# A Fourier filter with a two-layer network: the complex product M by three real products, and the units of a step behind its first layer

## The chip, the cores and the metric

The kernel runs on one core of one Trainium2 chip. The metric is the time of one execution in device microseconds. A core has the engines TensorE (PE in the profile, its weight loads PEld), VectorE (DVE), ScalarE (ACT), GpSimd (POOL) and SyncE (SP, which here only issues transfers), and 16 DMA engines. TensorE writes to PSUM only; GpSimd works on SBUF.

## The reference

The input x has 8 batches of 3008 rows and 256 columns. A Fourier transform along the rows is mixed by a complex 256 x 256 matrix, shrunk towards zero and transformed back; the result goes through a network with an ELU.

```python
X = np.fft.rfft(x, axis=1)
Yr = Xr @ w_r - Xi @ w_i + b_r
Yi = Xr @ w_i + Xi @ w_r + b_i
Yr = np.sign(Yr) * np.maximum(np.abs(Yr) - lam, 0.0)   # lam = 0.01, Yi alike
y = np.fft.irfft(Yr + 1j * Yi, n=3008, axis=1)
h = y @ w_in                                           # 256 -> 2048
g = np.where(h > 0.0, h, np.exp(np.minimum(h, 0.0)) - 1.0)
out = g @ w_out                                        # 2048 -> 256
```

## The kernel before

**The transform.** 3008 is 47 x 64, so the transform is done in two stages of matmuls each way. For one batch there are five kinds of units. A (6 of them, `unit_A`) is the 64-point stage out of x, which lies in the three tiles `xts`; its result goes to DRAM (tile DA) and comes back in another order as Z (`load_Z`). X (8, `unit_X`) is the 47-point stage, giving XT, real and imaginary parts apart. M (12, `unit_M` with `m_group`) is the complex product with `w_r`, `w_i` for 128 frequencies: four matmuls of 512 columns against `wcat_r` = [w_r, w_i] and `wcat_s` = [-w_i, w_r], then the bias (VectorE, tile yb), the clip and the subtraction (GpSimd, tiles clip and Y), which are the shrinking. B (6, `unit_B`) and Y (8, `unit_Y`) are the two stages back, again with DRAM between them (tile DB, loaded as Bs by `load_Bs`); Y leaves yT, which the network reads. A, X, B and Y are evacuated from PSUM by ScalarE.

**The network.** It goes in steps of 512 rows and 256 of the 2048 hidden columns, 47 steps to a batch (PER), 376 in all. `front` is the first layer (four matmuls, tile hps) and the exponential on ScalarE (tile Et): in one piece, in two halves, or as relu and exponential where the step has an M unit (L737, L738). `elu` takes the minimum of Et with 1: on GpSimd in halves (L763) in steps with no unit, on VectorE (L765) in steps with units other than M, and not at all with M, where the relu does its work. `finish_elu` puts it together with hps into gT on VectorE (L751, L753). `back` is the second layer of the step two before (LAG = 2): eight matmuls of 256 columns in f32 into ps_o, copied out every eighth step (tile osb).

**The order** is written out by hand, and each engine works through its instructions in that order. `plan(b)` gives a batch's 47 steps two lists: units of the next batches (f0) and other work (f1, such as loads of x on GpSimd's queue and of Z and Bs on SyncE's). In each step the loop calls the units of f0, `front`, `finish_elu` for the step before, f1, `elu` and `back`. In step 3 of batch 0 f1 has a `gate` (L599): a one-column copy on GpSimd that waits for a part of Z and so holds back the loads of x that follow it on that queue.

**PSUM.** Units share one buffer (psF, tag fps), which in some steps with no unit also holds an hps; hps has two more buffers (psH), ps_o two (psO). So a unit waits for the evacuation of the one before it, and the first layer of a step for gT of the step two before.

**SBUF.** The three gT buffers are larger than their tiles, which start 0, 32 and 16 bytes into them (`shifted`); the rows of `w_out_r` have 16 unused elements behind them (`E + 16`). Ahead of the steps GpSimd also copies the weights into `wcat_r` and `wcat_s` (L521 to L524) while VectorE makes the matrices of the transform (L488 and its neighbours). Batch 0 runs its units, and batch 1 its A units, before the first step, with VectorE and ScalarE sharing them (`first_M`, L221, keeps the product as it is).

Of the kernel before, what the change touches and what calls it, by code (L numbers as in the profile page):

```python
# [23 lines left out]
NJ = 24  # L24
# [5 lines left out]
def kernel(  # L30
# [31 lines left out]
    wcat_s = constp.tile([P, 2, 2 * D], BF16, name="wcat_s")  # L62
    w_in_s = constp.tile([P, 2, DFF], BF16, name="w_in_s")
    w_out_p = constp.tile([P, NFT, E + 16], F32R, name="w_out_r")
    w_out_r = w_out_p[:, :, 0:E]
    bias_bc = constp.tile([P, 2 * D], F32, name="bias_bc")
    bias_p = constp.tile([P, 2 * D], BF16, name="bias_p")
# [62 lines left out]
    def unit_A(b, u, alone=False, on_dve=False, ahead=False):  # L130
        ci, uu = u // 2, u % 2
        if uu == 0:
            if ahead and ci > 0:
                A_of[b, ci] = shifted(ci - 1, 8 * D, BF16, "A").rearrange("p (n d) -> p n d", d=D)
# [72 lines left out]
    def unit_M(b, q, i):  # L207
        if i == 0:
            mps_of[b, q] = unit_ps("mps", False)
        yb, clip = m_group(b, q, i, mps_of[b, q][:, i, :])  # L210
        nc.gpsimd.tensor_scalar(clip[:], yb, LAM, -LAM, ALU.min, ALU.max)  # L211
        nc.gpsimd.tensor_tensor(Y_of[b, q][:, i, :], yb, clip[:], ALU.subtract)  # L212
# [101 lines left out]
    with tc.tile_pool(name="stagep", bufs=1) as stagep:  # L314
# [35 lines left out]
        w_r_f = row("w_r_f", [P, 2, D])  # L350
        w_i_f = row("w_i_f", [P, 2, D])
# [217 lines left out]
    SHIFT = (0, 32, 16)  # L569

    def shifted(k, n_, dt, name):

        k %= 3
        o = SHIFT[k] * n_ // (8 * TB)
        w_ = n_ + 64 * n_ // (8 * TB)
        t = late1.tile([P, w_], dt, name=name, tag=f"gT{k}")
        return t[:, o : o + n_]
# [31 lines left out]
    load_w_out(0)  # L609
    nc.vector.tensor_scalar(w3[:], v3[:], CMAGIC, -CMAGIC, ALU.add, ALU.add)  # L610
# [134 lines left out]
    def finish_elu():  # L745
        for i, hps, Et, whole, halves in late_elu:
            gT = shifted(i + 2, 2 * TB, F32R, "gT").rearrange("p (s t) -> p s t", s=2)
# [9 lines left out]
    def elu(i, hps, Et, on_pool, on_act):  # L757

        E_ = Et[:]
        if on_pool:  # L760
# [3 lines left out]
        elif not on_act:  # L764
            nc.vector.tensor_scalar(E_, E_, 1.0, -1.0, ALU.min, ALU.add)  # L765
        late_elu.append((i, hps, Et, on_pool or on_act, on_pool))
# [44 lines left out]
    def plan(b):  # L811
# [4 lines left out]
        mid = [("X", u) for u in range(8)] + [  # L816
# [13 lines left out]
        for t, u in enumerate(seq, lead):  # L830
# [9 lines left out]
            if u == ("A", 1):  # L840
                f1[t] += [(load_Bs, (n1, w)) for w in range(4)]
# [68 lines left out]
```

## Time and profile before

| | |
|---|---|
| three timed runs | 917.59, 918.97, 920.98 us; median 918.97 us |
| the profiled execution, first to last instruction (its span) | 916.2 us, 2.8 under the median |
| granted TensorE clock, mean | 0.997 |
| busy: PE, DVE, ACT, POOL | 898.2, 718.1, 696.8, 313.4 us |
| DMA | 106.24 MB, mean 116 GB/s |

The time of the profiled execution is not given apart from its span; so times are worked out on the span, and 2.8 us are put to them for the median of the runs. In the lines of the profile, a group has its source line, engine, operation, output and inputs, shape and count, then the busy time in us and the mean duration in ns, then the time that the engine was idle before it and what ended that. A line of the timeline has its start and duration in us. PE durations contain a latency in which the next matmul already runs, so the distance from start to start is what a matmul occupies.

### The profile page before, as it was taken

How to read it: one execution, taken by the hardware profiler on the slowest of the kernel's cores; microseconds unless marked ns; L12 is line 12 of the kernel's file. 1: busy time of each engine (PE TensorE's matmuls, PEld its weight loads, DVE VectorE, ACT ScalarE, POOL GpSimd, SP SyncE). 2: the span in 40 equal slices, each digit the busy share in tenths (PEclk: the TensorE clock that was granted, in tenths of full speed). 3: DMA queues.
4: the chain of work that ended last, by engine and by line, in shares of the span. 5: the costliest groups of instructions: out<-in, count | busy, mean ns of one | idle time of the engine just before them, and what ended most of it. 6: DMA issues, size and time to landing. Idle time of an engine off the chain costs nothing.

```text
span 916.2 us, 17270 instructions
## 1 busy us (share of the span) xinstructions
PE 898.2 (98%) x6721; PEld 655.8 (72%) x6721; DVE 718.1 (78%) x891; ACT 696.8 (76%) x850; POOL 313.4 (34%) x438
## 2 busy tenths in 40 slices
PE   8889999999999999999999999999999999999997
PEld 3447667876678766886678766787667866777775
DVE  8759778887788777887788877888778877778775
ACT  6658778778778778787787788878877877766664
POOL 6600440323321342405404153033332134343664
PEclk9999999999999999999999999999999999999999
DMA  8997026621284214732266032752228111321011
GB/s 264 310 264 230 24 71 182 210 63 53 70 233 135 71 47 135 191 113 75 65 192 200 24 94 60 218 160 70 70 71 229 30 42 47 87 76 47 26 46 46
DMA packets 90670, 106.24 MB, mean 116 GB/s; under 512 B 5270, under 2 KB 81308, under 8 KB 87228
## 3 DMA queue, kind: packets, MB, share of 16 engines
q1 hardware_dynamic: 84332, 77.62, 30.3%
q0 software_dynamic: 5968, 27.26, 9.0%
q8 instruction: 52, 0.85, 0.4%
q10 hardware_dynamic: 288, 0.26, 0.1%
q14 instruction: 30, 0.25, 0.1%
HBM read 55.32 MB, written 49.81 MB: 115 GB/s over the span
## 4 chain that ended last, share of the span: by engine, by line
PE 88%; DMA 3%; ACT 3%; DVE 3%; issue 1%; SPq 1%; POOL 0%; ACTq 0%; DVEq 0%; POOLq 0%
PE ps_o L784 36%; PE hps L726 34%; PE mps L193 9%; PE xps L176 2%; PE yps L283 2%; PE bps L245 2%; PE aps L145 2%; DMA Bs<-DB 1%; DMA DA<-A 1%; ACT Et L737 1%; ACT Bz L258 1%; SPq L802 0%; DMA xt<-in_x_dram 0%; DVE gT L751 0%; DMA DB<-Bz 0%
## 5 line engine op out<-in xcount | busy, mean ns | idle before, releaser
L784 PE MATMUL ps_o<-w_out_r,gT 128*128 128x256 f32 x3008 | 482.5, 303 | 0.1
L784 PEld LDWEIGHTS ps_o<-w_out_r,gT 128*128 128x128 f32 x3008 | 406.8, 189 | 50.0 <-DVE osb L795 1.0
L726 PE MATMUL hps<-yT,w_in_s 128*128 128x512 bf16 (+4 forms) x1728 | 390.0, 353 | 3.3 <-DVE gT L753 2.5
L751 DVE SCALAR_TENSOR_TENSOR gT<-Et,hps 128x512 fp32r<-128x512 f32 (+1 forms) x272 | 222.8, 848 | 76.3 <-POOL Et L763 39.3
L753 DVE SCALAR_TENSOR_TENSOR gT<-hps,Et 128x1024 fp32r<-128x1024 f32 x198 | 242.1, 1223 | 18.0 <-DMA DA<-A 2.6
L726 PEld LDWEIGHTS <-w_in_s 128*128 128x128 bf16 x1728 | 141.7, 98 | 130.9 <-issue 23.5
L740 ACT ACTIVATE Et<-hps 128x1024 f32<-128x1024 f32 x198 | 203.9, 1030 | 14.3 <-PE hps L726 8.0
L763 POOL TENSOR_SCALAR Et<-Et 128x512 f32<-128x512 f32 x187 | 111.3, 614 | 224.9 <-ACT Et L735 224.9
L765 DVE TENSOR_SCALAR Et<-Et 128x1024 f32<-128x1024 f32 x198 | 137.0, 692 | 49.5 <-ACT Et L740 42.2
L211 POOL TENSOR_SCALAR clip<-yb 128x512 f32<-128x512 f32 x84 | 51.6, 614 | 319.5 <-DVE yb L203 282.1
L735 ACT ACTIVATE Et<-hps 128x512 f32<-128x512 f32 x188 | 102.1, 595 | 65.1 <-PE hps L726 65.1
L737 ACT ACTIVATE Et<-hps 128x1024 f32<-128x1024 f32 x84 | 86.3, 1027 | 72.6 <-PE hps L726 72.1
L212 POOL TENSOR_TENSOR Y<-yb,clip 128x512 bf16<-128x512 f32 x84 | 107.2, 1276 | 7.0
L738 ACT ACTIVATE Et<-Et 128x1024 f32<-128x1024 f32 x84 | 88.8, 1057 | 2.7
L203 DVE TENSOR_TENSOR yb<-mps,bias_bc 128x512 f32<-128x512 f32 x89 | 61.4, 689 | 36.8 <-PE mps L193 29.8
L128 ACT CAST XT<-xps 128x768 bf16<-128x768 f32 x61 | 48.7, 799 | 16.4 <-PE xps L176 16.4
L128 ACT CAST yT<-yps 128x752 bf16<-128x752 f32 x63 | 49.6, 788 | 14.6 <-PE yps L283 14.5
L193 PE MATMUL mps<-wcat_r,XT 128*128 128x512 bf16 x192 | 58.1, 383 | 0.8 <-DVE XT L126 0.4
L128 ACT CAST A<-aps 128x1024 bf16<-128x1024 f32 x45 | 45.5, 1013 | 16.3 <-PE aps L145 14.6
L193 PE MATMUL mps<-wcat_s,XT 128*128 128x512 bf16 x192 | 57.1, 379 | 0.0
L193 PEld LDWEIGHTS <-XT 128*128 128x128 bf16 x384 | 30.8, 98 | 29.9 <-DVE XT L126 0.7
L258 ACT CAST Bz<-bps 128x1024 bf16<-128x1024 f32 x46 | 46.0, 1000 | 2.6 <-PE bps L245 2.6
(110 smaller groups left out, 412.0 us busy)
## 6 DMA issues: line engine op xcount, KB each, us to landing
xt<-in_x_dram POOLq DMA_DIRECT2D x21, 1024.0 KB, 7.1
out_dram<-osb SPq DMA_DIRECT2D x158, 128.0 KB
Bs<-DB SPq DMA_DIRECT2D x32, 384.0 KB
DA<-A SPq DMA_DIRECT2D x21, 512.0 KB
DB<-Bz SPq DMA_DIRECT2D x21, 512.0 KB
Z<-DA SPq DMA_DIRECT2D x7, 1152.0 KB
Z<-DA SPq DMA_DIRECT2D x11, 384.0 KB
xt<-in_x_dram POOLq DMA_DIRECT2D x6, 512.0 KB, 6.2
```

The source lines that it names most:

```text
L128: nc.scalar.copy(dst, src)
L193: nc.tensor.matmul(ps, lhsT=XT[:, dt, c, o : o + P], rhs=wm[:, dt, :], start=(not biased and m == 0 and dt == 0), stop=(m == 1 and dt == 1),)
L212: nc.gpsimd.tensor_tensor(Y_of[b, q][:, i, :], yb, clip[:], ALU.subtract)
L726: nc.tensor.matmul(hps[:, s, c0:c1], lhsT=w_in_s[:, dt, ft * P : ft * P + P], rhs=yT_of[b][:, dt, t0 : t0 + c1 - c0], start=(dt == 0), sto ...
L735: nc.scalar.activation(E_[:, s], hps[:, s], AF.Exp)
L737: nc.scalar.activation(E_, hps[:], AF.Relu, scale=-1.0)
L740: nc.scalar.activation(E_, hps[:], AF.Exp)
L751: nc.vector.scalar_tensor_tensor(o, e, -1.0, h, ALU.add, ALU.max)
L753: nc.vector.scalar_tensor_tensor(o, h, 0.0, e, ALU.max, ALU.add)
L763: eng.tensor_scalar(E_[:, s], E_[:, s], 1.0, 0.0, ALU.min, ALU.max)
L765: nc.vector.tensor_scalar(E_, E_, 1.0, -1.0, ALU.min, ALU.add)
L784: nc.tensor.matmul(po[q][:, i_ % 2, :], lhsT=gT[:, s, i_ * P : i_ * P + P], rhs=w_out_r[:, ft, :], start=(ft == 0 and i_ % 2 == 0), stop=( ...
```

## The change

- **M by three real products**, batches 1 to 7. `unit_D` makes Xd = Xr - Xi (128 frequencies, 256 columns). `unit_M` multiplies Xd by w_i, Xr by w_r - w_i and Xi by w_r + w_i: six matmuls of 256 columns in place of four of 512. Kb = (first product + b_r) is added to the two others on VectorE, which gives the real part and, but for b_i - b_r (tile `bias_d`, added on GpSimd), the imaginary one. The sums of the weights (tile `wsum`) and `bias_d` are made once, on GpSimd, before the first step. Xd for the next unit is made on GpSimd, or on VectorE where the next step has an M too.
- **Order in a step**: `front` comes first and the units of f0 behind it; `finish_elu` now belongs to the same step, at its end. gT of step i is thus given to VectorE in step i and not in i + 1.
- **Order of the units** (`plan`): Y, A or empty steps are put between M units, in batches 5 and 6 behind nearly each, in batch 0 none but B; X starts two steps earlier; the loads of x are at steps 1, 4, 7 in batches 1 to 5, and as before at 3, 8, 13 in batch 0. The first Y units of the next batch come at fixed steps (`due`).
- **Minimum**: on GpSimd in halves wherever neither the two steps before nor the step behind has an M (210 steps for 94), also in steps with X, A, Y or B units; on VectorE in the steps near an M (82 for 198); none in steps with M (84).
- **No padding**: `w_out_r` is dense, and gT starts at its buffer's start (`ring`). `w_r_f` and `w_i_f` lie in the buffers of Y.

```diff
@@ -60,10 +60,11 @@
     M4 = constp.tile([4 * K1, 2 * N1], BF16, name="M4")
     wcat_r = constp.tile([P, 2, 2 * D], BF16, name="wcat_r")
     wcat_s = constp.tile([P, 2, 2 * D], BF16, name="wcat_s")
+    wsum = constp.tile([P, 2, 2, D], BF16, name="wsum")
     w_in_s = constp.tile([P, 2, DFF], BF16, name="w_in_s")
-    w_out_p = constp.tile([P, NFT, E + 16], F32R, name="w_out_r")
-    w_out_r = w_out_p[:, :, 0:E]
+    w_out_r = constp.tile([P, NFT, E], F32R, name="w_out_r")
     bias_bc = constp.tile([P, 2 * D], F32, name="bias_bc")
+    bias_d = constp.tile([P, D], F32, name="bias_d")
     bias_p = constp.tile([P, 2 * D], BF16, name="bias_p")
     lam_n = constp.tile([P, 1], F32, name="lam_n")
     hpi = constp.tile([P, 1], F32, name="hpi")
@@ -131,7 +132,7 @@
         ci, uu = u // 2, u % 2
         if uu == 0:
             if ahead and ci > 0:
-                A_of[b, ci] = shifted(ci - 1, 8 * D, BF16, "A").rearrange("p (n d) -> p n d", d=D)
+                A_of[b, ci] = ring(ci - 1, 8 * D, BF16, "A").rearrange("p (n d) -> p n d", d=D)
             elif alone:
                 A_of[b, ci] = wk4.tile([P, 8, D], BF16, name="A", tag="Bs")
             else:
@@ -204,12 +205,45 @@
         clip = wk2.tile([P, 2 * D], F32, name="clip", tag="clip")
         return yb, clip
 
-    def unit_M(b, q, i):
+    Xd_of = {}
+
+    def unit_D(b, k, eng):
+
+        if k >= NJ // 2:
+            return
+        Xd_of[b, k] = wk2.tile([P, 2, P], BF16, name="Xd", tag="Xd")
+        XT, o = XT_of[b], k * P
+        eng.tensor_tensor(
+            Xd_of[b, k][:], XT[:, :, 0, o : o + P], XT[:, :, 1, o : o + P], ALU.subtract
+        )
+
+    def unit_M(b, q, i, eng):
+
+        k = 2 * q + i
+        XT, Xd, o = XT_of[b], Xd_of.pop((b, k)), k * P
+        ps = unit_ps("mps", False)
+        kp = ps[:, 1, 0:D]
+        for lhs, rhs, dst in (
+            (lambda dt: Xd[:, dt], lambda dt: wcat_r[:, dt, D : 2 * D], kp),
+            (lambda dt: XT[:, dt, 0, o : o + P], lambda dt: wsum[:, 0, dt], ps[:, 0, 0:D]),
+            (lambda dt: XT[:, dt, 1, o : o + P], lambda dt: wsum[:, 1, dt], ps[:, 0, D : 2 * D]),
+        ):
+            for dt in range(2):
+                nc.tensor.matmul(dst, lhsT=lhs(dt), rhs=rhs(dt), start=dt == 0, stop=dt == 1)
         if i == 0:
-            mps_of[b, q] = unit_ps("mps", False)
-        yb, clip = m_group(b, q, i, mps_of[b, q][:, i, :])
-        nc.gpsimd.tensor_scalar(clip[:], yb, LAM, -LAM, ALU.min, ALU.max)
-        nc.gpsimd.tensor_tensor(Y_of[b, q][:, i, :], yb, clip[:], ALU.subtract)
+            Y_of[b, q] = wk3.tile([P, 2, 2 * D], BF16, name="Y", tag="Y")
+        yb = wk3.tile([P, 2 * D], F32, name="yb", tag="yb")
+        clip = wk2.tile([P, 2 * D], F32, name="clip", tag="clip")
+        Kb = wk2.tile([P, D], F32, name="Kb", tag="Kb")
+        nc.vector.tensor_tensor(Kb[:], kp, bias_bc[:, 0:D], ALU.add)
+        nc.vector.tensor_tensor(
+            yb[:].rearrange("p (c d) -> p c d", c=2), ps[:, 0].rearrange("p (c d) -> p c d", c=2),
+            Kb[:].unsqueeze(1).to_broadcast([P, 2, D]), ALU.add,
+        )
+        unit_D(b, k + 1, eng)
+        nc.gpsimd.tensor_tensor(yb[:, D : 2 * D], yb[:, D : 2 * D], bias_d[:], ALU.add)
+        nc.gpsimd.tensor_scalar(clip[:], yb[:], LAM, -LAM, ALU.min, ALU.max)
+        nc.gpsimd.tensor_tensor(Y_of[b, q][:, i, :], yb[:], clip[:], ALU.subtract)
 
     held = []
 
@@ -347,8 +381,7 @@
         NV = K1 // 2
         v3 = wk2.tile([P, NV, N2], F32, name="Bz", tag="Bz")
         w3, a3 = (wk2.tile([P, NV, N2], F32, name="A", tag="A") for _ in range(2))
-        w_r_f = row("w_r_f", [P, 2, D])
-        w_i_f = row("w_i_f", [P, 2, D])
+        w_r_f, w_i_f = (wk3.tile([P, 2, D], F32, name=nm, tag="Y") for nm in ("w_r_f", "w_i_f"))
 
 
         nc.scalar.activation(dume[:], busy[:, 0:1], AF.Sin, bias=0.0, scale=0.0)
@@ -566,15 +599,10 @@
     late2 = ctx.enter_context(tc.tile_pool(name="late2", bufs=2))
     late3 = ctx.enter_context(tc.tile_pool(name="late3", bufs=3))
     late1 = ctx.enter_context(tc.tile_pool(name="late1", bufs=1))
-    SHIFT = (0, 32, 16)
-
-    def shifted(k, n_, dt, name):
-
-        k %= 3
-        o = SHIFT[k] * n_ // (8 * TB)
-        w_ = n_ + 64 * n_ // (8 * TB)
-        t = late1.tile([P, w_], dt, name=name, tag=f"gT{k}")
-        return t[:, o : o + n_]
+
+    def ring(k, n_, dt, name):
+
+        return late1.tile([P, n_], dt, name=name, tag=f"gT{k % 3}")[:]
 
     w_in_v = moe_w_in.rearrange("(c p) f -> p c f", p=P)
     w_out_v = moe_w_out.rearrange("(t p) e -> p t e", p=P).bitcast(F32R)
@@ -607,6 +635,9 @@
     for ci in range(3):
         load_x(1, ci)
     load_w_out(0)
+    nc.gpsimd.tensor_tensor(wsum[:, 0], w_r_f[:], w_i_f[:], ALU.subtract)
+    nc.gpsimd.tensor_tensor(wsum[:, 1], w_r_f[:], w_i_f[:], ALU.add)
+    nc.gpsimd.tensor_tensor(bias_d[:], bias_bc[:, D : 2 * D], bias_bc[:, 0:D], ALU.subtract)
     nc.vector.tensor_scalar(w3[:], v3[:], CMAGIC, -CMAGIC, ALU.add, ALU.add)
     nc.vector.tensor_tensor(w3[:], v3[:], w3[:], ALU.subtract)
     nc.scalar.copy(bias_p[:], brow[:])
@@ -744,7 +775,7 @@
 
     def finish_elu():
         for i, hps, Et, whole, halves in late_elu:
-            gT = shifted(i + 2, 2 * TB, F32R, "gT").rearrange("p (s t) -> p s t", s=2)
+            gT = ring(i + 2, 2 * TB, F32R, "gT").rearrange("p (s t) -> p s t", s=2)
             for s in range(2) if halves else (slice(0, 2),):
                 o, h, e = gT[:, s], hps[:, s], Et[:, s]
                 if whole:
@@ -754,16 +785,16 @@
             g_of[i] = gT
         late_elu.clear()
 
-    def elu(i, hps, Et, on_pool, on_act):
+    def elu(i, hps, Et, min_on, halves):
 
         E_ = Et[:]
-        if on_pool:
+        if min_on == "pool":
             for s in range(2):
                 eng = nc.vector if i == n - 1 and s == 0 else nc.gpsimd
                 eng.tensor_scalar(E_[:, s], E_[:, s], 1.0, 0.0, ALU.min, ALU.max)
-        elif not on_act:
+        elif min_on == "dve":
             nc.vector.tensor_scalar(E_, E_, 1.0, -1.0, ALU.min, ALU.add)
-        late_elu.append((i, hps, Et, on_pool or on_act, on_pool))
+        late_elu.append((i, hps, Et, min_on != "dve", halves))
 
     def back(i, split):
         blk, fp = divmod(i, NPAIR)
@@ -813,20 +844,37 @@
         f0 = [[] for _ in range(PER)]
         f1 = [[] for _ in range(PER)]
         n1, n2 = b + 1, b + 2
-        mid = [("X", u) for u in range(8)] + [
-            ("M", 0, 0), ("M", 0, 1), ("M", 1, 0), ("M", 1, 1), ("B", 0), ("M", 2, 0),
-            ("M", 2, 1), ("B", 1), ("M", 3, 0), ("M", 3, 1), ("B", 2), ("M", 4, 0),
-            ("M", 4, 1), ("B", 3), ("M", 5, 0), ("M", 5, 1), ("B", 4),
-            ("A", 0), ("B", 5), ("A", 1), ("A", 2), ("A", 3), ("A", 4),
-        ]
+        lead = int(b == 0)
+        early = 6 if b == 0 else 4
+        seq = [("y", u) for u in range(2, early)]
+        rest_ = []
         if n1 < B:
-            lead, seq = int(b == 0), [("y", u) for u in range(2, 6)] + mid
-            seq.insert(20 if b else 4, ("y", 6))
-            seq.insert(24 if b else 5, ("y", 7))
-            xs = (3, 8, 13)
-            seq += [("A", 5), ("n", 0), ("n", 1)] if b else [("n", 0), ("n", 1), ("A", 5)]
+            due = 37 + b
+            seq += [("X", u) for u in range(8)]
+            fill = [("y", u) for u in range(early, 8)]
+            if n2 < B:
+                fill += [("A", u) for u in range(6)]
+            else:
+                fill += [("-",)] * 6
+            room = max(0, min(10, due - 5 - (b > 0) - lead - len(seq) - 17))
+            fill, rest_ = fill[:room], fill[room:]
+            cut = [-1, 11, 0, 4, 8, 2, 6, 10, 1, 11][: len(fill)]
+            fill = fill[::-1]
+            seq += [fill.pop() for c in cut if c < 0]
+            for k in range(12):
+                seq.append(("M", k // 2, k % 2))
+                if k % 2 and k > 1:
+                    seq.append(("B", k // 2 - 1))
+                for c in cut:
+                    if c == k:
+                        seq.append(fill.pop())
+            seq.append(("B", 5))
+            k = due - lead - len(seq)
+            seq += rest_[:k] + [("-",)] * (k - len(rest_))
+            seq += [("n", 0), ("n", 1)] + rest_[k:]
         else:
-            lead, seq = 0, [("y", u) for u in range(2, 8)]
+            seq += [("y", u) for u in range(early, 8)]
+        xs = (3, 8, 13) if b == 0 else (1, 4, 7)
         for t, u in enumerate(seq, lead):
             if u[0] == "y":
                 f0[t].append(put("Y", b, u[1]))
@@ -835,10 +883,15 @@
             elif u[0] == "A":
                 if n2 < B:
                     f0[t].append(put("A", n2, u[1]))
-            else:
+            elif u[0] == "M":
+                near = seq[t - lead + 1][0] == "M"
+                f0[t].append((unit_M, (n1, *u[1:], nc.vector if near else nc.gpsimd)))
+            elif u[0] != "-":
                 f0[t].append(put(u[0], n1, *u[1:]))
-            if u == ("A", 1):
-                f1[t] += [(load_Bs, (n1, w)) for w in range(4)]
+            if u == ("X", 7):
+                f1[t + 1].append((unit_D, (n1, 0, nc.gpsimd)))
+            if u == ("B", 5):
+                f1[t + (0 if b == 0 else 1)] += [(load_Bs, (n1, w)) for w in range(4)]
             if u == ("A", 5) and n2 < B:
                 f1[t] += [(load_Z, (n2, s0, s1)) for s0, s1 in ((0, 8), (8, NS))]
         if b == 0:
@@ -861,18 +914,20 @@
             free = not used[r]
             bare = bare + 1 if free else 0
             calm = free and (i >= n - 2 or (r + 2 < PER and not used[r + 1] and not used[r + 2]))
+            on_act = any(f is unit_M for f, a in f0[r])
+            near = any(f is unit_M for k in range(max(0, r - 2), min(PER, r + 2)) for f, a in f0[k])
+            min_on = "act" if on_act else "dve" if near or i == 0 else "pool"
+            halves = min_on == "pool"
+            h = front(i, calm and bare % 3 == 2, on_act, halves)
             for f, a in f0[r]:
                 f(*a)
-            on_act = any(f is unit_M for f, a in f0[r])
-            h = front(i, calm and bare % 3 == 1, on_act, free and i > 0)
-        finish_elu()
-        if i < n:
             for f, a in f1[r]:
                 f(*a)
             split = i > LAG and (i - LAG) % NPAIR == NPAIR - 1
             if split:
                 back(i - LAG, True)
-            elu(i, *h, free and i > 0, on_act)
+            elu(i, *h, min_on, halves)
+            finish_elu()
         else:
             split = False
         if i >= LAG and not split:
```

## The prediction

> **What bounds the kernel now.** I read the page first (engines, then the chain), then the groups with shapes kept apart, then the timeline of one M step, and last the timeline and the single lines of what GpSimd does.
>
> ```profile
> PE 898.2 (98%) x6721; PEld 655.8 (72%) x6721; DVE 718.1 (78%) x891; ACT 696.8 (76%) x850; POOL 313.4 (34%) x438
> PE 88%; DMA 3%; ACT 3%; DVE 3%; issue 1%; SPq 1%; POOL 0%; ACTq 0%; DVEq 0%; POOLq 0%
> ```
>
> TensorE is busy 98% of the span and is 88% of the chain that ended last: every stage but the first 57 us is as long as its matmuls. GpSimd, a third busy, is on no part of the chain. The price of a matmul comes from the groups by shape:
>
> ```profile
> L784 PE MATMUL ps_o<-w_out_r,gT 128*128 128x256 f32 x3008 | 482.5, 303 | 0.1
> L726 PE MATMUL hps<-yT,w_in_s 128*128 128x512 bf16 x1280 | 331.6, 381 | 3.3 <-DVE gT L753 2.5 <-ACT yT L128 0.5
> L212 POOL TENSOR_TENSOR Y<-yb,clip 128x512 bf16<-128x512 f32 x84 | 107.2, 1276 | 7.0
> L726 PE MATMUL hps<-yT,w_in_s 128*128 128x256 bf16 x64 | 8.3, 273 | 0.0
> ```
>
> A duration has a fixed latency in it; 512 against 256 columns differ by 108 ns, which is what 256 columns occupy. One M step in the timeline:
>
> ```profile
> 200.98 0.60 PE L193 MATMUL mps<-wcat_r,XT 128*128 128x512 bf16 x2
> 201.85 1.03 PE L726 MATMUL hps<-yT,w_in_s 128*128 128x512 bf16 x4
> 202.05 0.69 DVE L203 TENSOR_TENSOR yb<-mps,bias_bc 128x512 f32<-128x512 f32 x1 [0.87 <-PE mps L193]
> 202.53 1.29 PE L784 MATMUL ps_o<-w_out_r,gT 128*128 128x256 f32 x8
> 202.66 1.21 DVE L751 SCALAR_TENSOR_TENSOR gT<-Et,hps 128x1024 fp32r<-128x1024 f32 x1
> 202.84 0.61 POOL L211 TENSOR_SCALAR clip<-yb 128x512 f32<-128x512 f32 x1 [0.18 <-DVE yb L203]
> 202.91 1.03 ACT L737 ACTIVATE Et<-hps 128x1024 f32<-128x1024 f32 x1 [0.57 <-PE hps L726]
> 203.53 1.28 POOL L212 TENSOR_TENSOR Y<-yb,clip 128x512 bf16<-128x512 f32 x1
> 203.66 0.60 PE L193 MATMUL mps<-wcat_r,XT 128*128 128x512 bf16 x2
> ```
>
> The step goes from 200.98 to 203.66: four M matmuls 0.87, first layer 0.68, second layer 1.13, with no gap. In the same way a bare step is 1.81, one with Y 2.16, X 2.16, B 2.36, A 2.29. So a shorter M pays in full as long as nothing else comes late. What can come late is GpSimd:
>
> ```profile
> 60.41 0.69 DVE L765 TENSOR_SCALAR Et<-Et 128x1024 f32<-128x1024 f32 x1 [2.58 <-ACT Et L740]
> 60.76 0.38 POOL L599 CAST gate<-Bs 96x1 f32<-96x1 bf16 x1 [15.86 <-DMA Bs<-DB]
> 76.95 0.18 POOL L599 CAST gate<-Z 96x1 f32<-96x1 bf16 x1 [14.88 <-DMA Z<-DA]
> L488 DVE TENSOR_SCALAR M<-M,c x4: 228/408/650, 19.7 to 20.9; 96x24 bf16<-96x24 bf16 x4
> ```
>
> Two things are to be seen. The gate of batch 0 holds the GpSimd queue for 14.88 us, until Z lands at 76.95. And VectorE's minimum and a GpSimd instruction exclude each other: a gate that takes 0.18 alone takes 0.38 beside L765 and ends 0.04 after it, and the L488 instructions take 0.23 alone and up to 0.65 while GpSimd copies (L521, L522), ending with these copies.
>
> **Part 1, the three products.** 84 units change from 4 matmuls of 512 columns (0.864 at 216 ns) to 6 of 256 (0.654 at 109 ns): 0.210 x 84 = **17.6 us less**. The two extra weight loads per unit lie under the matmuls, as those of the first layer do; if they did not, L784's case bounds it: it costs 30 ns more than bf16 of its width (303 against 273), 6 x 0.03 x 84 = 15 us. I take nothing, since these weights are bf16 like those of L726.
>
> **Part 2, the gate.** The plan of batch 0 has the gate and a load of x in the second list of step 3, ahead of that step's minimum. Before, that minimum was on VectorE; now step 3 is "far from M", so its two halves queue on GpSimd behind the gate. Z's load starts where it did (67.67, when A has been written), so the gate still ends at 77.1, the issue of one load at 78.05, the halves (0.6 each) at 79.3, gT's second half (0.68) at 80.0. The first layer of step 5 needs the buffer that gT of step 3 frees (two buffers), so it starts at 80.0. Before it started at 71.15, with one more Y unit (0.34) done. Lost: 8.9 + 0.3 = **9.2 us**. After TensorE's idle time at 56 us the granted clock was 0.5 from 57.7 to 61.1; the same again loses half of 3.4, **1.7 us**. Behind the gate there also wait the minima of step 4 and later; they follow at 1.2 us each, in time.
>
> **Part 3, minimum against subtraction.** An M unit now puts on VectorE a 256-wide add out of PSUM (Kb), the 512-wide add (0.69) and gT, and on GpSimd the bias add (256), clip, subtraction and the difference Xd for the next unit. No row has the 256-wide ones: Kb lies between 0.25 (a 64-wide DVE line) and 0.69; 0.53 per 512 elements (1.22 for 1024, 0.69 for 512) gives 0.42. The GpSimd add lies between 0.61 (one-input, 512) and 1.28 (two-input, 512); half of the latter gives 0.66. Take time zero at an M's first matmul, behind a B step. That step's minimum is ready 1.45 after its unit began (exponential 0.39 behind the first layer's last start, 1.03, 0.03), and gT follows to 3.47, so VectorE is free 3.47 - 2.36 = 1.11 into the M step. Kb starts at 1.03, yb ends at 2.24 (0.42 + 0.10 + 0.69). GpSimd: add from 2.34, clip from 3.08, subtraction 3.77 to 5.05. The next step begins at 2.46, and its minimum, kept on VectorE because it is near M, is ready at 3.91: 0.14 us too late. It waits to 5.05, and gT ends at 7.07 instead of 5.93. The next M starts at 4.75 (A between them); its adds could start at 5.61 and now start at 7.0, yb ends at 8.2, and as psF has one buffer the unit behind starts at 8.25 instead of 7.21. **1.04 us lost.** In the pair that follows TensorE is late itself, the minimum arrives in the clip, waits 0.4, and nothing is lost; then it recurs. Behind A the same sum has the minimum 0.09 too late; behind Y, 0.06 early. M units with B or A before and a VectorE minimum behind, every second one of a chain counted: batches 1 to 6 have 2, 2, 3, 4, 4, 4 = 19; 19 x 1.04 = **20 us** (batch 0 has none). Bounds: nothing (the margins are about 0.1 us), and some 35 us if those behind Y lose too.
> The Trainium skill, SBUF — State Buffer, section Terms, says of the port pair of VectorE and GpSimd that it is locked exclusively for a whole instruction and that the loser blocks fully. The rows agree but for one: L523 on GpSimd is shown to end at 23.89 inside L611, a two-input VectorE instruction (23.44 to 24.40); by the rule this part stays at 20 us, by that row the two would share and it would be nothing.
>
> **Part 4, smaller ones.** Where M follows M (15 units) Xd is on VectorE between yb and gT, and the next M's first weight load waits for it: no such row, 0.23 (L488) to 0.69 (L203), I take 0.42; that makes the next unit 0.15 to 0.4 late, less where Xd is shorter: **3 us** (0 to 6). Units stand behind the first layer, so ScalarE evacuates after the exponential: for X or Y with halves 0.39 + 1.09 + 0.70 + 0.05 = 2.22 against a step of 2.16, A 2.43 against 2.29; late by 0.06 and 0.15 in every second step, 92 X/Y and 21 A steps: 0.03 x 92 + 0.075 x 21 = **4 us**. In seven B steps with an output copy before, that copy stood ahead of the evacuation and cost 0.36; now it stands behind: **-2.5 us**. B5 to the next Y falls from 11.4 to 10.5, 10.0 and 9.6 us in batches 3 to 5; 9.1 was short by 1.2 in batch 6 before, so some 10.3 are needed: **0.8 us** more. At nothing: the weight sums on GpSimd (2 x 1.28 + 0.66) lie in its wait of 4.5 us before the first clip; at most 0.5 if VectorE holds them up. The earlier loads of x put 0.6 us ahead of a minimum that has 1 us to spare. Z's loads keep 9 steps, 17 us, in batch 0 and 12 later, against 9.3 from issue to landing. Without padding: f32 costs 30 ns over bf16 both at L784 and at L145 (413 against 381), whose operand xt was never padded; nothing, 2 us either way.
>
> **Sum.** 916.2 - 17.6 + 9.2 + 1.7 + 20 + 3 + 4 - 2.5 + 0.8 = 934.8. The median of the runs is 2.8 over the profiled span, so **937.6 us**. This case's own range, with 11 to 28 us for part 3, is 928 to 946.
>
> **Rivals.** (a) The port is exclusive but the minimum gets in ahead of the subtraction: a margin of 0.1 us speaks for it, the sum against: 937.6 - 20 = 917.6, no change. (b) VectorE and GpSimd share the port, so neither the minimum nor Xd is held up; decided by whether an L765 inside a subtraction still takes 0.69. L523 speaks for it, the gates and L488 against; 937.6 - 23 = 914.6, faster by 0.5%. (c) The units behind Y lose as well, if yb is 0.06 earlier than I put it: 15 more, 953. (d) The second layer's f32 weights load under the last matmul ahead of them, so far always 512 columns, now often a 96-column one of X or Y that lasts 42 ns. Spacing in the second layer is 118 ns, so up to 0.076 shows in 118 steps: 9 us, 946.6. For it: nothing here has that order; against: TensorE was never seen waiting for a weight load.
> The Trainium skill, TensorE: Matmul & The Clock Gate, section LDWEIGHTS, gives columns / 1.2 as the load's ns; an estimate from it is 107 ns, thus 65 exposed, 7.7 us; no run here shows it.
>
> **Chances.** Forecast 0.43, (a) 0.20, (b) 0.14, (c) 0.12, (d) 0.11. About 0.5% (914.4 to 923.6 is no change) is what a measurement of this kernel can tell. The small terms of part 4 are known to some 4 us, so of (b) 0.09 fall on faster and 0.05 on the same, of (a) 0.06 and 0.14: faster 0.15, the same 0.19, slower 0.66. From 910 to 951 holds (a), the forecast, (d) and most of (b) and leaves out half of (c) and the tails.
>
> **What would show it.** In the profile after: M matmuls of 256 columns start 0.109 apart; a gap of about 9 us on TensorE near 71 to 80 us with GpSimd in the gate, and a half clock behind it; minima in steps next to M that last 1.5 us and more, inside subtractions, and units behind them that wait for yb about 1 us. Minima at 0.69 throughout mean (a) or (b); no gap at 71 us takes 10.9 off; a gap ahead of each second layer behind X means (d).

## The result and the profile after

The changed kernel takes 946.4 us (median of 4 runs, 946.1 to 948.0), the kernel before 918.8 beside it: 1.031 times as long, 95% interval 1.029 to 1.033. The profiled span is 944.9 us, with a mean granted clock of 0.988. The minimum is now at L796 (VectorE) and L794 (GpSimd), gT at L782 and L784, the first layer at L757, the second at L815, the M matmuls at L232.

The page of the changed kernel, engines and chain:

```profile
PE 901.4 (95%) x6889; PEld 663.9 (70%) x6889; DVE 722.6 (76%) x992; ACT 697.0 (74%) x966; POOL 581.7 (62%) x824
...
PE 74%; DVE 17%; issue 3%; ACT 3%; DMA 1%; POOL 1%; DVEq 0%; ACTq 0%; SPq 0%; POOLq 0%
```

TensorE was 88% of the chain and is 74%; VectorE went from 3% to 17%. GpSimd's busy time nearly doubled. The groups by shape (count, busy us, mean ns, idle time ahead and what ended it):

```profile
L815 PE MATMUL ps_o<-w_out_r,gT 128*128 128x256 f32 x3008 | 448.7, 292 | 0.6 <-ACT osb L826 0.4 <-DVE gT L782 0.2
L757 PE MATMUL hps<-yT,w_in_s 128*128 128x512 bf16 x1280 | 333.2, 383 | 22.7 <-DVE gT L784 11.5 <-DVE gT L782 9.4 <-ACT yT L129 0.8
...
L246 POOL TENSOR_TENSOR Y<-yb,clip 128x512 bf16<-128x512 f32 x84 | 117.3, 1397 | 7.0
L796 DVE TENSOR_SCALAR Et<-Et 128x1024 f32<-128x1024 f32 x82 | 89.4, 1090 | 14.8 <-ACT Et L771 12.4
L216 POOL TENSOR_TENSOR Xd<-XT 128x256 bf16<-128x256 bf16 x67 | 54.3, 813 | 0.0
L232 PE MATMUL mps<-wsum,XT 128*128 128x256 bf16 x336 | 50.4, 273 | 0.0
```

The minimum, 0.69 us before, has a mean of 1.09. The first layer waited 3.3 us in all before; now it waits 20.9 us for gT alone. An M matmul lasts 273 ns like any bf16 matmul of 256 columns, and its starts are 0.109 us apart.

Cut into steps, from the first matmul of one first layer to that of the next, the traces have these medians in us (the one or two Y steps at the start that have no second layer yet are left out; the count stands behind the sum):

| step with | before | after | sum before | sum after |
|---|---|---|---|---|
| M | 2.689 | 2.480 (smallest 2.460) | 226.6 (84) | 223.9 (84) |
| Y | 2.168 | 2.214 | 135.0 (60) | 147.6 (61) |
| X | 2.169 | 2.214 | 122.5 (56) | 126.6 (56) |
| B | 2.447 | 2.547 | 102.9 (42) | 109.7 (42) |
| A | 2.292 | 2.305 | 82.9 (36) | 86.1 (36) |
| no unit | 1.821 | 1.810 | 174.2 (95) | 173.6 (94) |

The first matmul of the first layer is at 62.7 us; it was at 57.4. So 5.3 us are lost ahead of the steps; and the M steps, whose matmuls are 17.6 us shorter, are only 2.7 us shorter in all.

The timeline shows the three places. First the start (L638 to L640 are the weight sums):

```profile
28.23 1.55 POOL L638 TENSOR_TENSOR wsum<-w_r_f,w_i_f 128x512 bf16<-128x512 f32 x1
28.70 1.63 DVE L651 TENSOR_TENSOR yb<-yb,bias_p 64x512 f32<-64x512 f32 x1
...
31.78 0.96 DVE L127 CAST XT<-xps 128x768 bf16<-128x768 f32 x1
32.79 0.80 PE L177 MATMUL xps<-M,Z 96*128 96x96 bf16 x8 [2.23 <-DVE XT L127]
```

The sums take GpSimd from 28.23 to 32.32; L651 ends 0.55 us behind the end of the first, and L650 to L652 take 1.50, 1.63 and 1.37 us. The evacuation of XT behind them is 3 us late, TensorE waits 2.23 us for it, and the X matmuls behind that run slower (0.80 for eight, elsewhere 0.51; the granted clock is 0.50 from 30 to 34 us). Second, the gate of batch 0:

```profile
82.00 0.18 POOL L627 CAST gate<-Z 96x1 f32<-96x1 bf16 x1 [11.87 <-DMA Z<-DA]
...
83.12 2.37 POOL L794 TENSOR_SCALAR Et<-Et 128x512 f32<-128x512 f32 x4
83.81 1.28 DVE L782 SCALAR_TENSOR_TENSOR gT<-Et,hps 128x512 fp32r<-128x512 f32 x2 [8.98 <-POOL Et L794]
85.15 1.87 PE L757 MATMUL hps<-yT,w_in_s 128*128 128x512 bf16 x4 [7.08 <-DVE gT L782]
```

GpSimd stands in the gate, the minima (two of each step) queue behind it, gT waits 8.98 us, TensorE 7.08, and its next four matmuls take 1.87 in place of 1.04: half the clock (0.50 granted from 85.15 to 87 us). Third, a step next to M:

```profile
808.68 1.27 POOL L246 TENSOR_TENSOR Y<-yb,clip 128x512 bf16<-128x512 f32 x1
808.72 1.77 DVE L796 TENSOR_SCALAR Et<-Et 128x1024 f32<-128x1024 f32 x1
...
810.60 1.23 DVE L784 SCALAR_TENSOR_TENSOR gT<-hps,Et 128x1024 fp32r<-128x1024 f32 x1
...
811.87 1.02 PE L757 MATMUL hps<-yT,w_in_s 128*128 128x512 bf16 x4 [0.63 <-DVE gT L784]
```

The minimum comes 0.04 us behind the start of the subtraction (808.68 to 809.95), ends 0.54 behind its end, and pushes gT, which the first layer of two steps on waits for; Kb and yb of the M unit (L238, L239) queue behind gT on VectorE. In the trace 64 of the 82 minima start inside a GpSimd instruction; they end 0.55 us behind the end of that instruction in the median. Of all 82, 50 take over 0.8 us, the longest 1.81. TensorE's waits show where this arrives (total, times, longest; a wait counts only beyond the latency that a matmul's duration contains):

```profile
PE hps L757 <- DVE gT L784: 11.5, 23, 2.0
...
PE aps L146 <- DVE yb L239: 0.8, 4, 0.2
```

It is the first layer that waits for gT; units wait little for yb.

### The profile page after: what moved, and what is told of

Its sections match the earlier page's. It is cut to its first block, busy times and chain, and to the rows that moved or that the text cites. A ratio compares the mean times of both kernels' runs of the same rounds, so it can differ in the third digit from the quotient of the medians.

```text
span 944.9 us, 18191 instructions
## 1 busy us (share of the span) xinstructions
PE 901.4 (95%) x6889; PEld 663.9 (70%) x6889; DVE 722.6 (76%) x992; ACT 697.0 (74%) x966; POOL 581.7 (62%) x824
## 4 chain that ended last, share of the span: by engine, by line
PE 74%; DVE 17%; issue 3%; ACT 3%; DMA 1%; POOL 1%; DVEq 0%; ACTq 0%; SPq 0%; POOLq 0%
PE ps_o L815 31%; PE hps L757 29%; DVE Et L796 4%; DVE gT L784 4%; PE mps L232 4%; PE bps L279 2%; PE xps L177 2%; ACT Et L771 2%; DVE yb L239 2%; PE aps L146 2%; PE yps L317 2%; DVE gT L782 1%; PE mps L194 1%; DVE Kb L238 1%; DVE osb L826 1%
## 5 line engine op out<-in xcount | busy, mean ns | idle before, releaser
L782 DVE SCALAR_TENSOR_TENSOR gT<-Et,hps 128x512 fp32r<-128x512 f32 (+1 forms) x504 | 371.7, 772 | 158.2 <-POOL Et L794 140.7
L815 PE MATMUL ps_o<-w_out_r,gT 128*128 128x256 f32 x3008 | 448.7, 292 | 0.6 <-ACT osb L826 0.4
L757 PE MATMUL hps<-yT,w_in_s 128*128 128x512 bf16 (+4 forms) x1728 | 391.8, 354 | 22.7 <-DVE gT L784 11.5
L815 PEld LDWEIGHTS ps_o<-w_out_r,gT 128*128 128x128 f32 x3008 | 386.5, 189 | 26.1 <-issue 8.9
L794 POOL TENSOR_SCALAR Et<-Et 128x512 f32<-128x512 f32 x419 | 249.5, 614 | 187.7 <-ACT Et L766 187.7
L766 ACT ACTIVATE Et<-hps 128x512 f32<-128x512 f32 x420 | 228.3, 596 | 121.7 <-PE hps L757 121.7
L757 PEld LDWEIGHTS <-w_in_s 128*128 128x128 bf16 x1728 | 134.4, 98 | 124.0 <-issue 26.7
L244 POOL TENSOR_TENSOR yb<-yb,bias_d 128x256 f32<-128x256 f32 x84 | 61.6, 733 | 111.1 <-DVE yb L239 111.0
L768 ACT ACTIVATE Et<-hps 128x1024 f32<-128x1024 f32 x84 | 86.3, 1027 | 48.4 <-PE hps L757 48.0
L771 ACT ACTIVATE Et<-hps 128x1024 f32<-128x1024 f32 x82 | 84.2, 1027 | 42.5 <-PE hps L757 42.5
L784 DVE SCALAR_TENSOR_TENSOR gT<-hps,Et 128x1024 fp32r<-128x1024 f32 x82 | 100.4, 1225 | 8.3 <-PE hps L757 0.5
L796 DVE TENSOR_SCALAR Et<-Et 128x1024 f32<-128x1024 f32 x82 | 89.4, 1090 | 14.8 <-ACT Et L771 12.4
L239 DVE TENSOR_TENSOR yb<-mps,Kb 128x512 f32<-128x512 f32 x84 | 58.1, 692 | 7.6 <-DVE Kb L238 0.5
L216 POOL TENSOR_TENSOR Xd<-XT 128x256 bf16<-128x256 bf16 x67 | 54.3, 813 | 0.0
L232 PE MATMUL mps<-wsum,XT 128*128 128x256 bf16 x336 | 50.4, 273 | 0.0
```

The source lines that it names most:

```text
L232: nc.tensor.matmul(dst, lhsT=lhs(dt), rhs=rhs(dt), start=dt == 0, stop=dt == 1)
L757: nc.tensor.matmul(hps[:, s, c0:c1], lhsT=w_in_s[:, dt, ft * P : ft * P + P], rhs=yT_of[b][:, dt, t0 : t0 + c1 - c0], start=(dt == 0), sto ...
L766: nc.scalar.activation(E_[:, s], hps[:, s], AF.Exp)
L771: nc.scalar.activation(E_, hps[:], AF.Exp)
L782: nc.vector.scalar_tensor_tensor(o, e, -1.0, h, ALU.add, ALU.max)
L784: nc.vector.scalar_tensor_tensor(o, h, 0.0, e, ALU.max, ALU.add)
```

## The experiments

**Alone, each of the three places.** The minimum of the first steps back on VectorE:

```diff
-            min_on = "act" if on_act else "dve" if near or i == 0 else "pool"
+            min_on = "act" if on_act else "dve" if near or i < 9 else "pool"
```

> The changed kernel with the minimum of steps 1 to 8 of batch 0 back on VectorE, so that no minimum is queued on GpSimd behind the gate of step 3. Theory (the gate of step 3 holds that step's minimum, which holds its gT, which holds the first layer of step 5, and a half clock follows): the 10.0 us step of the changed kernel shrinks to about 2.2 us and the half clock behind it goes, 9 to 10 us less, 936 to 938 us. Rival (the step waits for the data that the gate waits for, not for the minimum): the long step stays, 946 us.

Measured: 936.5 us (1.017 of before, 1.014 to 1.021), 9.9 less than the changed kernel. The step that took 10.02 us takes 2.23. The first theory holds for the step; a half clock is still granted here, but ahead of it, from 67.5 to 74.3 us.

The weight sums later on GpSimd:

```diff
-    nc.gpsimd.tensor_tensor(wsum[:, 0], w_r_f[:], w_i_f[:], ALU.subtract)
-    nc.gpsimd.tensor_tensor(wsum[:, 1], w_r_f[:], w_i_f[:], ALU.add)
-    nc.gpsimd.tensor_tensor(bias_d[:], bias_bc[:, D : 2 * D], bias_bc[:, 0:D], ALU.subtract)
...
+    nc.gpsimd.tensor_tensor(wsum[:, 0], wcat_r[:, :, 0:D], wcat_s[:, :, 0:D], ALU.add)
+    nc.gpsimd.tensor_tensor(wsum[:, 1], wcat_r[:, :, 0:D], wcat_r[:, :, D : 2 * D], ALU.add)
+    nc.gpsimd.tensor_tensor(bias_d[:], bias_bc[:, D : 2 * D], bias_bc[:, 0:D], ALU.subtract)
     load_Bs(0, 0)
```

> The changed kernel with the three weight-sum instructions (wsum twice, bias_d) moved on GpSimd from before the first bias work to behind the last M unit of the prologue that needs none of them, made there from the bf16 weights. Theory (the sums on GpSimd stretch VectorE's bias_p instructions, which delay the evacuation of XT, for which TensorE waits and loses its clock): bias_p back to 0.42 to 0.75 us each, the first matmul of the first layer at about 57.4 us instead of 62.7, time 941 us. Rival (the 5 us at the start come from the other order of the prologue's units): 946 us.

Measured: 942.1 us (1.025, 1.0225 to 1.027), 4.3 less; the first layer starts at 57.5 us, 5.2 earlier, and the step at the gate is longer instead (11.16 us for 10.02). The timeline with nothing on GpSimd beside VectorE but issues (L648 is L651 above):

```profile
27.43 0.69 DVE L648 TENSOR_TENSOR yb<-yb,bias_p 64x512 f32<-64x512 f32 x1
...
28.67 0.96 DVE L127 CAST XT<-xps 128x768 bf16<-128x768 f32 x1
```

The three instructions take 0.42, 0.69 and 0.49, 1.60 us for 4.50, and the evacuation is 3.1 us earlier.

The minimum near M replaced by an instruction of the same length that reads PSUM:

```diff
-            nc.vector.tensor_scalar(E_, E_, 1.0, -1.0, ALU.min, ALU.add)
+            if i < 9:
+                nc.vector.tensor_scalar(E_, E_, 1.0, -1.0, ALU.min, ALU.add)
+            else:
+                nc.vector.tensor_scalar(E_[:, 0], hps[:, 0], 1.0, -1.0, ALU.min, ALU.add)
```

> The changed kernel, in which the VectorE minimum of the steps near an M unit is replaced, from step 9 of batch 0 on, by a VectorE instruction of the same place, waits and order that reads 512 columns of the first layer's result out of PSUM and writes them to half of Et; the minimum itself is left out there. It takes about as long (0.69 us). Theory (VectorE's minimum, which reads and writes SBUF alone, can't run beside GpSimd's two-input subtraction): the replacement takes 0.69 us throughout, where the minimum took 1.09 on the mean, the waits for yb near M go, 20 to 25 us less, 922 to 926 us. Rival (VectorE and GpSimd have simply more to do near M, and the order of their queues makes units late): 946 us, within 3. A second rival (it is the f32 weight load behind short matmuls): 946 us as well, with the replacement at 0.69 us.

Measured: 924.5 us (1.006, 1.004 to 1.008), 21.9 less. Its page, the engines, the chain and the group:

```profile
PE 894.1 (97%) x6889; PEld 662.6 (72%) x6889; DVE 695.1 (75%) x992; ACT 696.7 (76%) x966; POOL 559.5 (61%) x824
...
PE 89%; DVE 5%; issue 2%; ACT 2%; DMA 1%; POOL 1%; DVEq 0%; ACTq 0%; SPq 0%; POOLq 0%
...
L799 DVE TENSOR_SCALAR Et<-hps 128x512 f32<-128x512 f32 x81 | 55.9, 690 | 15.3 <-ACT Et L771 12.7
```

Of the 81 replacements 67 lie beside a GpSimd instruction, and the longest takes 0.693 us. GpSimd gets 22 us shorter too, though its instructions are the same: the exclusion cost both. An instruction on VectorE of the same length and in the same place, but out of PSUM, costs nothing, so it is not the load of the two engines' queues. The replacement handles half as many columns in the same time, though; whether its source or its lower speed keeps it free, these runs don't separate. In the changed kernel gT at L784, which takes one operand from PSUM and one from SBUF, isn't held up either: 60 of the 82 start inside a GpSimd instruction, and the longest takes 1.227 us, as in the kernel before.

**The order alone.** Units ahead of the first layer again, `finish_elu` left where the change put it:

```diff
-            h = front(i, calm and bare % 3 == 2, on_act, halves)
             for f, a in f0[r]:
                 f(*a)
+            h = front(i, calm and bare % 3 == 2, on_act, halves)
```

> The changed kernel with a step's units put ahead of its first layer again, as in the kernel before; all else stays. Theory (the order costs something at every X, Y and B step, either because the second layer's first f32 weight load shows behind a short matmul or because ScalarE evacuates behind the exponential): Y and X steps from 2.214 back to 2.168 us and B from 2.547 to 2.447, 2.8 + 2.6 + 4.2 = 9 to 10 us less, 937 us. If it is the exponential alone, only the steps with a late evacuation gain, 4 us less, 942 us. Rival (with the units first the M units' adds meet gT on VectorE in another way and the loss near M grows): 946 to 956 us.

Measured: 994.0 us (1.0815, 1.0795 to 1.0835), 47.6 more: beyond both. The gain is there (X steps 2.147 us, the smallest Y step 2.134), but a B step has a median of 3.45. The waits of this kernel:

```profile
PE bps L279 <- DVE yb L239: 30.8, 26, 1.8
PE yps L317 <- DVE yb L239: 13.5, 15, 1.5
```

The unit behind M waits for yb. An M unit now stands 0.86 us (a first layer) earlier, but on VectorE its Kb still stands behind gT of the step before. In the kernel before, with units first, gT of the step before stood behind yb, since `finish_elu` came a step later. So the two moves belong together, and this run doesn't show the old order's price with three products.

That gain shows what the order costs at X: the same 20 matmuls take 2.214 us in the changed kernel and 2.147 in this one. In the single starts of the changed kernel, from the matmul ahead of the second layer to that layer's eighth, the median is 1.024 us behind a first-layer matmul of 512 columns and 0.923 behind X, Y and M alike. Less what the matmul ahead itself occupies (0.216 for the first layer, 0.042 for X, 0.041 for Y, 0.109 for M) that is 0.808, 0.881, 0.882 and 0.814: 0.07 us more behind a matmul of 94 or 96 columns, and next to nothing behind one that lasts 0.109. The groups of weight loads of the changed kernel have a reason at hand, a load of f32 lasts 189 ns and one of bf16 98; no run changes the load itself:

```profile
L815 PEld LDWEIGHTS ps_o<-w_out_r,gT 128*128 128x128 f32 x3008 | 386.5, 189 | 26.1 <-issue 8.9 <-ACT osb L826 1.4 <-DVE osb L826 1.1
L757 PEld LDWEIGHTS <-w_in_s 128*128 128x128 bf16 x1728 | 134.4, 98 | 124.0 <-issue 26.7 <-DVE gT L782 0.8
```

**The parts put together.** The first three edits at once:

> The changed kernel with all three edits together: the minimum of steps 1 to 8 of batch 0 on VectorE, the weight sums behind the prologue's M units, and, from step 9 of batch 0 on, the instruction out of PSUM in place of the minimum near M (which is left out there). Theory (three separate losses): they add up, 946.4 - 9.9 - 4.3 - 21.9 = 910.3 us, 2 either way. Rival (they share their gains, for instance because a step that is early waits for the next DMA): 918 us or more.

Measured: 910.5 us (0.991, 0.989 to 0.9925). The three losses add up to 0.2 us.

The old product in the new order, with the first two edits:

```diff
-        k = 2 * q + i
...
-        nc.gpsimd.tensor_tensor(yb[:, D : 2 * D], yb[:, D : 2 * D], bias_d[:], ALU.add)
+        ps = unit_ps("mps", False)
+        yb, clip = m_group(b, q, i, ps[:, 0, :])
```

> The changed kernel with the minimum of steps 1 to 8 on VectorE and the weight sums late, and with the four-matmul product of the kernel before in all batches, so no Xd, no Kb and no add on GpSimd; the order (units behind the first layer, M alternating) stays. Theory: TensorE gets 84 x 0.21 = 17.6 us longer, and the blocked minima near M go, because the step is longer and GpSimd and VectorE have 1.5 and 0.4 us less to do for an M: 932.2 + 17.6 - 21.9 = 928 us. By the other side the same: 918.8 of the kernel before plus the dearer X, Y and B steps of the new order (2.6 + 2.8 + 4.2) = 928. Rival (the minima are blocked by the subtraction all the same): 945 to 950 us.

Measured: 923.3 us (1.005, 1.003 to 1.006), 5 less than expected. Its group of minima on VectorE:

```profile
L774 DVE TENSOR_SCALAR Et<-Et 128x1024 f32<-128x1024 f32 x90 | 62.6, 696 | 32.0 <-ACT Et L749 32.0
```

With the old product in the same order 77 of the 90 minima lie beside nothing on GpSimd, 12 come into the last 0.2 us of a subtraction, and the longest takes 0.758 us. GpSimd has no add and no Xd to do, and the M step is 0.22 us longer; which of these keeps the two apart wasn't tried.

The kernel before without its padding:

```diff
-    w_out_p = constp.tile([P, NFT, E + 16], F32R, name="w_out_r")
+    w_out_p = constp.tile([P, NFT, E], F32R, name="w_out_r")
...
-        o = SHIFT[k] * n_ // (8 * TB)
-        w_ = n_ + 64 * n_ // (8 * TB)
+        o, w_ = 0, n_
```

> The kernel before without its padding: w_out and gT lie dense, nothing else is changed. Theory of the prediction (the padding is worth nothing): 919 us, 2 either way. Rival (the bare steps, 1.82 us before and 1.80 in the changed kernel, are shorter because the operands lie dense): 375 x 0.02 = 7.5 us less, 911 us. The contrary (the padding does avoid a cost): slower than 921 us.

Measured: 916.0 us, 0.997 of before (0.996 to 0.998): 3 us less, between the two theories. The bare steps have a median of 1.800 us (1.821 padded), those with units 6 to 32 ns less.

**What ends the wait.** The subtraction in two instructions, with the first two edits:

```diff
-        nc.gpsimd.tensor_tensor(Y_of[b, q][:, i, :], yb[:], clip[:], ALU.subtract)
+        for c in range(0, 2 * D, 256):
+            nc.gpsimd.tensor_tensor(
+                Y_of[b, q][:, i, c : c + 256], yb[:, c : c + 256], clip[:, c : c + 256], ALU.subtract
+            )
```

> The changed kernel with the minimum of steps 1 to 8 on VectorE, the weight sums late, and GpSimd's subtraction in two instructions of 256 columns instead of one of 512; all is computed. Theory (VectorE waits for the end of the GpSimd instruction in progress, not for the end of GpSimd's work): a minimum that comes 0.14 us into the subtraction waits 0.5 instead of 1.1 us, the lost microsecond of the M steps becomes 0.4 to 0.5, 10 to 14 us less than the 932.2 of the two first edits, 918 to 922 us; the longest L796 falls from 1.9 to about 1.3 us. Rival (GpSimd keeps the port from one instruction to the next): 932 us and more.

Measured: 917.9 us (0.999, 0.998 to 1.000), 14.3 less than 932.2 (that is 946.4 less 9.9 and 4.3; the kernel with the two first edits alone wasn't run, but the parts added up to 0.2 us). Its group of minima:

```profile
L799 DVE TENSOR_SCALAR Et<-Et 128x1024 f32<-128x1024 f32 x90 | 82.2, 913 | 15.4 <-ACT Et L774 12.6
```

The longest is 1.27 us. And in four instructions:

> As the kernel with the subtraction in halves (minimum of steps 1 to 8 on VectorE, weight sums late), with the subtraction in four instructions of 128 columns. Theory (VectorE waits for the end of the instruction in progress): a minimum waits at most 0.35 us for a subtraction, the clip of 0.6 is now the longest; halves gave 14.3 of the 21.9 us, quarters give 3 to 4 more, 914 us. Rival (what is left of the loss hangs on the clip, the bias add and Xd, and two more instructions make yb's chain on GpSimd longer): 917 to 920 us.

Measured: 913.8 us (0.994, 0.992 to 0.9955): 0.6% faster than the kernel before, the fastest here that computes everything. Its group of minima:

```profile
L799 DVE TENSOR_SCALAR Et<-Et 128x1024 f32<-128x1024 f32 x90 | 76.1, 846 | 17.4 <-ACT Et L774 14.6
```

VectorE is let in at the end of the GpSimd instruction in progress: in both kernels, as in the changed one, a minimum that starts inside a GpSimd instruction ends 0.55 us behind it in the median. Shorter instructions make a shorter wait. The longest is still 1.22 us; the longest now start inside Xd, the bias add and the clip.

**Three tries to get back the X and Y steps.** Their units (`inner`) ahead of the last first-layer matmul:

```diff
+                if s == 1 and m == len(todo) - 1:
+                    for f, a in inner:
+                        f(*a)
                 nc.tensor.matmul(hps[:, s, c0:c1], ...)
+            if halves:
+                nc.scalar.activation(E_[:, s], hps[:, s], AF.Exp)
```

> The changed kernel in which an X or Y unit (not a Y behind an M) stands ahead of the last of its step's four first-layer matmuls instead of behind it; nothing else is changed, and ScalarE's evacuation stands ahead of the (second) exponential by this. Theory (the second layer's first f32 weights are loaded under the matmul ahead of them; behind a 96-column one 0.06 us shows): X steps from 2.214 to 2.147 us, those Y steps likewise, 56 x 0.067 + 45 x 0.06 = 6.5 us less, 940 us. Rival (the dearer X and Y steps come from ScalarE, which evacuates behind the exponential): the step shrinks only where the evacuation was late, 943 us or more, and the distance from the last matmul ahead of the second layer to its eighth keeps its 62 us/1000 too much.

> All edits that compute everything together: minimum of steps 1 to 8 on VectorE, weight sums late, subtraction in four, X and Y units ahead of the last first-layer matmul. Theory (the losses are separate): the quarters' time less 6.5 us, 907 to 909 us, faster than the kernel before by 1%. Rival (the X and Y steps' gain is taken back by a later wait): 914 us or more.

Measured: 1118.8 us (1.217, 1.215 to 1.220) and 1081.8 us (1.177, 1.175 to 1.179). The waits of the first:

```profile
PE hps L766 <- ACT Et L772: 146.3, 210, 1.2
```

The edit also put the first half's exponential between the matmuls of one tile hps, and the second half's matmuls wait for it. Neither run tells anything of the weight load. So once more with ScalarE's order kept (both exponentials, then the evacuation):

> The kernel with the subtraction in quarters (minimum of steps 1 to 8 on VectorE, weight sums late), in which the matmuls of an X or Y unit (not a Y behind an M) stand ahead of the last of the four first-layer matmuls; ScalarE's instructions keep their order, both exponentials and then the evacuation. So no exponential stands between first-layer matmuls, which in the two kernels before it made the last matmuls wait for the first exponential of the same tile. Theory (the second layer's first f32 weights show behind a 96-column matmul): X steps from 2.214 to 2.147 us, 913.8 - 6.5 = 907 us. Rival (the 0.067 us are ScalarE's late evacuation): X steps stay at 2.21 and the time at 914 us.

Measured: 941.5 us (1.0245, 1.023 to 1.026); X and Y steps take about 2.58. The timeline of this kernel from one X to the next:

```profile
195.80 0.50 PE L181 MATMUL xps<-M,Z 96*128 96x96 bf16 x8 [0.29 <-ACT XT L789]
...
196.55 1.09 ACT L782 ACTIVATE Et<-hps 128x512 f32<-128x512 f32 x2 [0.81 <-PE hps L775]
...
197.53 0.81 ACT L789 CAST XT<-xps 128x768 bf16<-128x768 f32 x1
...
198.38 0.50 PE L181 MATMUL xps<-M,Z 96*128 96x96 bf16 x8 [0.26 <-ACT XT L789]
```

A ring has closed: X, last first-layer matmul, two exponentials, evacuation, and the next X needs the one buffer for units: 2.58 us round. Both theories' times were missed. But where a first-layer matmul of 512 columns stands ahead of the second layer, the eighth comes 1.024 us behind it in this kernel as well, and 1.042 in the steps with X and Y (medians): of the 0.07 us some 0.055 are gone there, so most of it goes with the matmul ahead.

## Why the prediction was right, and where its sum was not

The verdict is the forecast one, and 946.4 lies in the range, 8.8 above 937.6. The two largest losses, the gate and the minima, were named and sized; the 8.8 come mostly from the weight sums, the order and the products, less the padding. The runs make a chain that gives each part its size: dense -3.0, new order +7.3 (923.3 - 916.0), three products with nothing held up -12.8 (910.5 - 923.3), minima against GpSimd +21.9, gate +9.9, weight sums +4.3. 918.8 and these are 946.4.

- **The three products, -17.6.** As priced: starts 0.109 us apart, the M steps of 910.5 and 923.3 sum to 208.0 and 225.0. The steps around gave back some 4 us (A 1.5, bare 1.4, Y 0.9); 3 were priced, for M units that wait for Xd on VectorE. Xd took 0.347 us there, but that wait explains little of it: ahead of M units the starts of these two kernels differ by 0.8 us in all, ahead of A units by 2.2. What gave the 4 us back wasn't tried.
- **The gate, 9.2 + 1.7.** Measured 9.9; the whole chain of part 2 is in the timeline, half clock included.
- **Minimum against subtraction, 20.** Measured 21.9. That minima are blocked by the subtraction is right, but they also come into the clip (26 of the 64) and the bias add (10), and the way from there to TensorE was mostly another. The prediction let the late gT hold up yb and, as there is one unit buffer, the unit behind, by about 1 us. TensorE's starts in the changed kernel and in the one with the instruction out of PSUM have the same order; from 122 us on their gaps differ by 21.6 us, of which 14.7 lie ahead of first layers (33 places) and 6.9 ahead of units (A 2.4, M 1.9, B 1.8, Y 0.8). The first layer waits for gT of the step two before, since hps has two buffers: the path that part 2 used and part 3 left out. Nor were there 19 losses of 1.04, but some 60 smaller ones (34 M steps lose 0.1 to 0.8 us, 11 B steps 0.1 to 0.3, 9 A steps 0.1 to 0.5). So the cause was foreseen, and that 20 comes so near 21.9 is in part luck. The Trainium skill, SBUF — State Buffer, section Terms (the port pair is locked for a whole instruction, and the loser blocks), is borne out: the 64 minima end 0.55 us in the median behind the instruction they came into. The instructions that read PSUM were not held up. The row L523 that spoke against it stays unexplained.
- **The weight sums "at nothing, at most 0.5".** This step failed: 4.3 us. The prediction had the exclusion in hand for part 3 and looked here only at what GpSimd itself was waiting for, not at the VectorE instructions beside it, on the path of XT.
- **Order: ScalarE's evacuation 4, output copies -2.5, DB 0.8.** 2.3 were priced, 7.3 measured, and the cause was not the one named. X steps are longer by the same 0.045 us each (lower quartile 2.213, upper 2.233), not every second one: rival (d), which came true beside the forecast, but only in part. By medians X and Y give 56 x 0.045 + 61 x 0.046 = 5.3 us against the padded kernel, for 9 in the rival; B gives 42 x 0.10 = 4.2 more, and the rival didn't have B. Between the old product in the new order and the dense kernel before, all B steps sum to 5.0 us more, X to 2.4, Y to 1.9. In the changed kernel the second layer's eighth matmul comes 1.118 us behind B's last (64 rows); why was not tried. The copies had nothing to give: the B steps before sum to 102.9, and 42 x 2.447 is 102.8. DB did not get dearer: TensorE waits 1.0 us for Bs, and waited 2.7. An estimate from the Trainium skill, TensorE: Matmul & The Clock Gate, section LDWEIGHTS, gave 65 ns exposed; 73 ns behind X and 74 behind Y were measured. The load that it puts at 107 ns lasts 189 for f32 and 98 for bf16 in this trace, so the agreement doesn't prove the load to be the reason.
- **Padding at nothing, 2 either way.** 3.0 us gained without it, 1 more than the bound.
- **Rivals (a) and (b)** fell with the minima of 1.09 us; (c) with 21.9 where it had 35.

## What to carry to other kernels

Before work is moved to GpSimd, list the VectorE instructions that read and write only SBUF beside it, in every stage, the setup too: each may wait for the end of a whole GpSimd instruction. If it must go there, cut it into short instructions or let VectorE's critical ones read PSUM. And when a tile is late, look at everything that waits for it: here two thirds of the minima's loss reached TensorE by the first layer's buffers, which the sum left out. When an order is turned round, look at which matmul now stands ahead of each long weight load, and at which instruction the in-order engines now meet first.

## What the runs showed of the hardware

- A VectorE instruction that reads PSUM and writes SBUF (128 x 512, 0.690 us) isn't held up by a two-input GpSimd instruction; one from SBUF to SBUF (128 x 1024) that takes as long alone was, up to 1.81. GpSimd pays as well: in the changed kernel its subtraction has a mean of 1.397 us and Xd of 0.813, with the instruction out of PSUM 1.280 and 0.673.
- Behind a matmul of 42 ns the second layer in f32 takes 0.07 us more; behind one of 109 ns that is gone. An f32 weight load of 189 ns fits this, but isn't shown to be the reason.
- Dense operands made the kernel before 3.0 us faster; the second layer's matmuls have a mean of 301 ns there for 303.
